# The first chunks of four batches at once, loaded by four-token rows, in a recurrence-and-expert kernel

## The chip, the cores and the metric

The kernel runs on one core of a Trainium2 chip. The metric is the device time of one execution in microseconds (us). The same kernel, run again, mostly agrees within a few tenths of a per cent. On some chips of this study it spread more, so every experiment was run beside the kernel before on its own chip, and the ratio to those runs counts. An execution over 1.5% longer than the fastest of its kernel is called slow, any other fast. The trace of one execution is read beside it. Its span, from the first to the last instruction, is mostly 1.7 to 2 us shorter than the device time (2.9 at most in these runs).

Engines: PE is TensorE (matmuls), DVE VectorE, ACT ScalarE, POOL GpSimd. SP issues transfers ("the sync queue"), and ACT and GpSimd have queues of their own.

## The reference, cut to what matters

```python
B, H, S, D = 4, 8, 768, 48            # float32 inputs; alpha in 0.8 .. 1.0
for t in range(S):
    state = alpha[:, :, t, :, None] * state + einsum('bhd,bhe->bhde', k[:, :, t], v[:, :, t])
    y[:, :, t] = einsum('bhd,bhde->bhe', q[:, :, t], state)
x = y.transpose(0, 2, 1, 3).reshape(3072, 384)
h = x @ w_in                           # 384 -> 2048
r = maximum(h, 0); out = (r * r) @ w_out   # 2048 -> 384
```

First comes a gated linear recurrence over time for each batch and head, then an expert layer with squared ReLU over all 3072 tokens.

## The kernel before

The recurrence is cut into chunks of 128 tokens, six for each batch, 24 in all. Within a chunk, cumulative products of alpha (a logarithm on ACT, a triangular matmul on PE, two exponentials on ACT) scale q and k. Masked scores times v give the part within the chunk, and a state carried from chunk to chunk gives the rest. The expert layer's matmuls keep PE busy from some 22 us on, and the later chunks are woven between them by a small scheduler that fixes the order of all instructions when the kernel is built.

The kernel before starts with the first four chunks of batch 0. Their alpha and q come in rows of four tokens (192 floats, 768 B) into tiles of 128 partitions, two transfers for each; k and v come chunk by chunk:

```python
slot_srcs = {n: a[0, :, 0:4 * P, :].rearrange("h (p j) d -> p h (j d)", j=4) for n, a in srcs}
LB = 5; LBV = 6                                   # buffers of the later tiles
...
def load_slots(nm, lo, hi):                       # half of the heads, all 128 partitions
    nc.sync.dma_start(out=slot[nm][:, lo:hi], in_=slot_srcs[nm][:, lo:hi])
...
def load_tile(nm):                                # v is cast to bf16 on its way in
    if nm == "vt": return loads.tile([P, H, D], BF16, name=nm, bufs=LBV)
    return loads.tile([P, H, D], FP32, name=nm)
... (nc.gpsimd if pool or nm == "vt" else nc.sync).dma_start(out=d[nm], in_=src[b, c])
...
def e_ps():                                       # state += kI^T v, chunk after chunk
    for p in range(NP): mm(st[:, p, :], lhsT=kI[:, 2*p:2*p+2, :], rhs=d["vt"][:, 2*p:2*p+2, :], ...)
def e_stm(): nc.vector.tensor_mul(st4, st4, bcast(ae, D))
def e_sb():  nc.scalar.copy(d["sbt"], d["st"])
...
def e_out(): nc.sync.dma_start(out=out_r[GT[g] + tt], in_=box["ob"])     # one transfer a tile
```

## Time and profile before

| | before |
|---|---|
| device time, median of the first three runs | 191.22 us (190.83 to 191.79) |
| span of the trace | 189.4 us |
| first expert matmul | 22.50 us |
| last expert matmul ends | 186.29 us |
| PE from the one to the other ("the stream") | 163.8 us |
| output after it ("the tail") | 3.1 us |

Three stretches add up to the span: the fill, the stream and the tail. The prediction below shows the lines for them. One more line belongs here, the granted clock of PE in 40 slices of 4.7 us (9 is full speed):

```profile
PEclk9998589999999999999999999999999999999999
```

The clock is low once, in the fourth to sixth slices, at the end of the fill.

### The profile page before, as it was taken

Reading aid. Unit: us, or ns where it says so; the run is one execution under the profiler, and the core shown is the slowest. Engines: PE = TensorE matmul, PEld = TensorE weight load, DVE = VectorE, ACT = ScalarE, POOL = GpSimd, SP = SyncE. Lnnn points to the kernel's source line nnn. Section 1 sums busy time; section 2 is a strip of 40 time slices with the busy share of each in tenths; the row PEclk is TensorE's granted clock in tenths of the full one; section 3 lists DMA queues with packets and bytes.
Section 4 is the critical chain, followed back from the end, with each engine's and each line's share of the span. In section 5 each row is a group of like instructions: output and inputs, shape, how many; then the busy total and the mean of one; then the engine's idle time right before and its main releaser. Section 6 shows DMA issues by size and latency. Waiting matters only on the chain.

```text
span 189.4 us, 5215 instructions
## 1 busy us (share of the span) xinstructions
PE 180.2 (95%) x1999; PEld 137.1 (72%) x1999; DVE 132.3 (70%) x335; ACT 126.7 (67%) x346; POOL 42.2 (22%) x78
## 2 busy tenths in 40 slices
PE   7864999999999999999999999999999999999993
PEld 2553778866878887777777787787787787777773
DVE  3167946754899795897886886886886886944411
ACT  3763459926778886678588588488588586565630
POOL 8967335023122233222021031041000000000000
PEclk9998589999999999999999999999999999999999
DMA  5999999899999999999959739739011011011112
GB/s 177 238 165 203 204 223 211 125 183 147 183 191 185 206 180 173 201 153 188 218 130 142 166 84 124 170 87 126 0 45 43 3 42 45 6 37 45 42 42 83
DMA packets 94280, 24.71 MB, mean 130 GB/s; under 512 B 85216, under 2 KB 93920, under 8 KB 94256
## 3 DMA queue, kind: packets, MB, share of 16 engines
q1 hardware_dynamic: 64992, 17.45, 44.8%
q0 software_dynamic: 29120, 6.88, 37.5%
q8 instruction: 15, 0.25, 0.6%
q14 instruction: 9, 0.07, 0.1%
q10 hardware_dynamic: 144, 0.05, 0.1%
HBM read 25.17 MB, written 4.72 MB: 158 GB/s over the span
## 4 chain that ended last, share of the span: by engine, by line
PE 87%; DMA 5%; SPq 3%; ACT 1%; DVE 1%; issue 1%; ACTq 0%; DVEq 0%
PE bank L226 78%; PE bank L229 7%; DMA kt<-in_k_dram 5%; PE st L226 2%; SPq L339 2%; SPq L319 1%; ACT r L668 1%; DVE st L578 1%; DVE sm L533 1%; ACT sb L583 0%; ACT xn L220 0%; DVE ob L736 0%; ACT ob L736 0%; ACT L_s L442 0%; DVE kI_s L474 0%
## 5 line engine op out<-in xcount | busy, mean ns | idle before, releaser
L668 ACT ACTIVATE r<-bank 128x256 bf16<-128x256 f32 (+1 forms) x160 | 64.7, 429 | 29.6 <-PE bank L226 28.2
L226 PE MATMUL bank<-xT_big,w_in_b 128*128 128x256 bf16 (+1 forms) x624 | 80.0, 266 | 0.1
L226 PE MATMUL bank<-w_out_b,gT 128*128 128x384 bf16 (+1 forms) x400 | 74.7, 320 | 0.0
L226 PEld LDWEIGHTS <-w_in_b 128*128 128x128 bf16 x624 | 53.8, 98 | 9.7 <-issue 0.5
L675 DVE TENSOR_TENSOR gT<-r 128x256 bf16<-128x256 bf16 (+1 forms) x160 | 47.6, 315 | 16.0 <-ACT r L668 14.4
L226 PEld LDWEIGHTS <-gT 128*128 128x128 bf16 x400 | 37.9, 98 | 15.8
L533 DVE TENSOR_TENSOR sm<-bank,utri_b 128x512 bf16<-128x512 f32 x40 | 25.3, 683 | 2.6 <-PE bank L226 2.5
L339 POOL DMA_DIRECT2D vt<-in_v_dram x24 | 21.3, 888 | 7.9 <-POOL vt L338 6.1
L338 POOL CAST vt<-kt 128x1 bf16<-128x1 f32 x18 | 4.7, 263 | 64.6 <-PE bank L226 41.8
L471 DVE TENSOR_TENSOR qA_s<-qt,A 128x384 bf16<-128x384 f32 x20 | 11.1, 556 | 9.5 <-ACT A L458 8.6
L218 DVE COPY qkT<-bank 128x1024 bf16<-128x1024 bf16 x20 | 13.8, 688 | 4.9 <-PE bank L229 4.9
L474 DVE TENSOR_TENSOR kI_s<-kt,Ainv 128x384 bf16<-128x384 f32 x24 | 13.3, 556 | 3.1 <-DMA kt<-in_k_dram 2.6
L709 ACT COPY ob<-bank 128x384 f32<-128x384 f32 x21 | 10.1, 480 | 8.1 <-PE bank L226 8.1
L226 PEld LDWEIGHTS <-qkT 64*128 64x128 bf16 (+1 forms) x260 | 10.4, 97 | 5.9 <-issue 2.5
L220 ACT CAST xn<-bank 128x384 bf16<-128x384 f32 x23 | 10.9, 480 | 4.2 <-PE bank L226 3.8
L583 ACT CAST sb<-st 128x384 bf16<-128x384 f32 x20 | 9.6, 478 | 5.7 <-DVE st L578 5.7
L458 ACT ACTIVATE A<-bank 128x384 bf16<-128x384 f32 x20 | 9.9, 496 | 2.4 <-PE bank L226 2.4
L229 PE MATMUL bank<-ident_bf,kI_s 128*128 128x128 bf16 x96 | 9.5, 223 | 2.1 <-DVE kI_s L474 2.1
L578 DVE TENSOR_TENSOR st<-st,ae_s 128x384 f32<-128x384 f32 x20 | 11.1, 556 | 0.0
L442 ACT ACTIVATE L_s<-at 128x384 bf16<-128x384 f32 x20 | 10.4, 521 | 0.0
L462 ACT ACTIVATE Ainv<-bank 128x384 bf16<-128x384 f32 x20 | 10.2, 510 | 0.0
L229 PE MATMUL bank<-ident_bf,qA_s 128*128 128x128 bf16 x96 | 9.3, 219 | 0.8 <-DVE qA_s L407 0.7
(78 smaller groups left out, 162.1 us busy)
## 6 DMA issues: line engine op xcount, KB each, us to landing
out_dram<-ob SPq DMA_DIRECT2D x23, 192.0 KB, 2.7
kt<-in_k_dram SPq DMA_DIRECT2D x21, 192.0 KB, 5.3
at<-in_alpha_dram SPq DMA_DIRECT2D x18, 192.0 KB, 4.8
qt<-in_q_dram SPq DMA_DIRECT2D x18, 192.0 KB, 4.7
vt<-in_v_dram POOLq DMA_DIRECT2D x24, 96.0 KB, 5.6
w_in_b<-in_moe_w_in_dram POOLq DMA_DIRECT2D x4, 384.0 KB, 11.0
w_out_b<-in_moe_w_out_dram POOLq DMA_DIRECT2D x4, 384.0 KB, 12.3
slot_at<-in_alpha_dram SPq DMA_DIRECT2D x2, 384.0 KB, 3.6
```

Source lines behind the costliest of these rows:

```text
L218: pin(nc.vector.tensor_copy(out, in_))
L220: pin(nc.scalar.copy(out, in_))
L226: pin(nc.tensor.matmul(*a, **kw))
L229: pin(nc.tensor.transpose(*a))
L339: pin((nc.gpsimd if pool or nm == "vt" else nc.sync).dma_start(out=d[nm], in_=src[b, c]))
L442: pin(nc.scalar.activation(L[:, :, 0:D], d["at"], AF.Ln))
L471: pin(nc.vector.tensor_mul(qA[:, :, 0:D], d["qt"], d["A"]))
L474: pin((nc.vector if mk.eng == "DVE" else nc.gpsimd).tensor_mul(kI[:, :, 0:D], d["kt"], d["Ai"]))
L533: pin(nc.vector.tensor_mul(d["sm"][:, hh], d["sc"][hh], (utri_p if first else utri_b).to_broadcast([P, NP, P])))
L578: pin(nc.vector.tensor_mul(st4, st4, bcast(ae, D)))
L668: pin(nc.scalar.activation(box["r"], box["ph"], AF.Relu))
L675: pin(nc.vector.tensor_mul(gT[g][:, f0:f0 + nf, 0:n], box["r"], box["r"]))
```

## The change

The four first chunks are now those of all four batches, which do not depend on each other, so the chain of states drops out of the fill. Alpha, q and k come with one transfer a batch, by four-token rows, and each batch fills 32 partitions. Scores are made for two batches by halves of the heads. After that the kernel goes batch by batch. The new token order of the first tiles is kept through to the output, which is put right by four output transfers a tile. The core of the diff (names, masks, scheduling ranks and most of the arithmetic cut):

```diff
-    slot_srcs = {n: a[0, :, 0:4 * P, :].rearrange("h (p j) d -> p h (j d)", j=4) for n, a in srcs}
+    NJ, PQ = 4, 32
+    rows = {n: a[:, :, 0:P, :].rearrange("b h (g j) d -> b g h (j d)", j=NJ) for n, a in srcs}
+    v_rows = v[:, :, 0:P, :].rearrange("b h (g j) d -> j g (b h) d", j=NJ)
+    SEQ = [(b, 0) for b in range(B)] + [(b, c) for b in range(B) for c in range(1, NCH)]
-    LB = 5
-    LBV = 6
+    LB = 4
...
+    def load_batch(nm, b, q, at):
+            pin(q.dma_start(out=slot[nm][b * PQ:(b + 1) * PQ], in_=rows[nm][b]))
+    def load_v(j, at):
+            pin(nc.sync.dma_start(out=v_0[j * PQ:(j + 1) * PQ]..., in_=v_rows[j]))
...
+    def load(s, pool):                     # later chunks: v in float32 too, on the same queue
+        for nm in ("at", "qt", "kt", "vt"):
+                pin((nc.gpsimd if pool else nc.sync).dma_start(out=C[s][nm], in_=srcs[nm][c, :, ...]))
...
+        def e_vb():                        # and cast by GpSimd
+            pin(nc.gpsimd.tensor_copy(d["vb"], d["vt"]))
...
-            pin(nc.sync.dma_start(out=out_r[GT[g] + tt], in_=box["ob"]))
+            if SEQ[GT[g] + tt][1] == 0:
+                for j in range(NJ):
+                    pin(nc.sync.dma_start(out=out_tile(GT[g] + tt)[j], in_=ob[j * PQ:(j + 1) * PQ]))
...
+    ld_at = [load_batch("at", b, nc.sync if b % 2 == 0 else nc.scalar, 0.9) for b in range(B)]
+    ld_qt = [load_batch("qt", b, nc.sync, 1.7) for b in range(B)]
+    ld_kt = [load_batch("kt", b, nc.sync, 1.7) for b in range(B)]
+    def hold():                            # the weights wait for the last k
+        pin(nc.gpsimd.tensor_copy(w_in_b[3 * PQ:P, 0, 0:1], slot["kt"][3 * PQ:P, 0, 0:1]))
```

## The prediction

> **What bounds the kernel now.** I read four views of the kernel before, in this order. First the page's shares of the chain of waits that ended last:
>
> ```profile
> PE 87%; DMA 5%; SPq 3%; ACT 1%; DVE 1%; issue 1%; ACTq 0%; DVEq 0%
> ```
>
> PE carries 87% of the chain, so most of the kernel cannot be shortened by taking a wait away. The chain in order of time tells where the other 13% lie (columns: start us, us, what):
>
> ```profile
> 3.47 2.81 SPq L339
> ...
> 6.33 9.01 DMA kt<-in_k_dram
> ...
> 15.84 0.56 DVE st L578
> 16.40 0.96 DVE sm L533 x2
> ...
> 18.09 0.49 ACT sb L583
> ...
> 22.50 15.27 PE bank L226 x139
> ```
>
> Up to 15.3 us the path is the third key tile's transfer; then comes the serial chain over the four chunks of batch 0 (state update on DVE, its copy on ACT, the next state matmul on PE), until 22.50 us. From there on the chain is PE with hardly a break to 186.31 us; 3.1 us of output follow. Third, the windows (stretch, length, busy us of PE, PEld, DVE, ACT, POOL, granted clock, DMA share, GB/s):
>
> ```profile
> 12.00:14.00 2.00, 1.23 (x20) 0.97 (x20) 1.23 (x3) 1.26 (x4) 0.77 (x1) 1.00 1.63 162
> 14.00:16.00 2.00, 0.57 (x14) 0.26 (x10) 0.64 (x2) 0.09 (x1) 1.46 (x2) 1.00 1.38 192
> 18.00:20.00 2.00, 1.84 (x20) 1.29 (x17) 2.00 (x5) 1.00 (x3) 0.75 (x1) 0.50 1.24 203
> 22.00:24.00 2.00, 1.99 (x25) 1.54 (x23) 1.91 (x4) 0.86 (x3) 0.76 (x1) 0.50 1.30 202
> 30.00:35.00 5.00, 5.00 (x51) 4.42 (x50) 3.06 (x8) 4.65 (x9) 1.28 (x2) 1.00 1.28 219
> ```
>
> PE starves at 14 to 16 us, its clock is then halved (second by second from about 17.9 to 24.7 us), and after that PE is full. Fourth, the timeline, where the first expert matmul and the speed of the stream are seen:
>
> ```profile
> 22.50 0.80 PE L226 MATMUL bank<-xT_big,w_in_b 128*128 128x256 bf16 x3
> ...
> 27.51 7.38 PE L226 MATMUL bank<-xT_big,w_in_b 128*128 128x256 bf16 x66
> ```
>
> So the time is: start of the expert stream (22.50) + work of PE from there (163.8) + tail (3.1) = 189.4 us of span; the device time of 191.22 lies 1.8 above it. The change can win only by an earlier start, less PE work in the stream, or fewer cold cycles.
>
> **What the Trainium skill says.** "TensorE: Matmul & The Clock Gate", Part 1, gives two states of the clock, half and full, switched by a free-running activity window of 3.4 us, and a warm matmul spacing of N/2.4 + 2.5 ns. The trace agrees: clock exactly 0.50 for 6.7 us (two windows), and 66 matmuls of 256 columns in 7.38 us less one drain, about 109 ns each. "DMA: Bandwidth & Descriptors", Specifications, asks for 512 B or more per piece; the trace shows 366 GB/s at 3 to 4 us with 768 B rows and 158 to 174 at 9 to 13 us with 192 B rows and casts. The same page's "Queues, rings and completion order" says that each DMA engine takes turns between the queues with work; the third key tile, issued at 6.33, landed only at 15.34 while GpSimd's queue was busy, which fits. "SBUF — State Buffer", "Door 1: The DMA port swizzle", says 32 (or 64) neighbouring partitions reach 8 of 16 ports. The new transfers are of 32 partitions each; no transfer of before is, so the trace cannot test it. It may cost them their speed where two of the same half run together.
>
> **The change part by part.**
>
> *Loads.* Alpha, q and k of all four first chunks come in 768 B rows, 4 x 196 KB each, 2.36 MB; v in 192 B rows, 0.79 MB, uncast. The weights are held until the last k landed. Two of the four alpha transfers are issued by ACT behind its table load (0.80 to 2.08 us). Before, an alpha transfer landed 3.3 to 4.0 us after issue, so all four are there at about 5.4 (before: 5.3). The queue on SP reuses eight semaphores, so each k transfer waits for an alpha and each v for a q to land. At 250 to 300 GB/s (estimate from the trace's 257 to 366 at 3 to 7 us, lowered for the ports) k is complete at 2.2 + 2.36/0.27 = 11 us, before 15.3. Then v at about 200 GB/s needs 4 us alone; from about 13 us the first weights share with it: v lands at about 16.5 to 17, the first quarter of w_in (393 KB) at about 17.
>
> *ACT.* From 5.4: 4 logarithms of 0.52 and 8 exponentials of 0.50 make 6.1 us, last one at 11.5. Before it was two of 0.84 and the same eight, ended 10.25.
>
> *DVE.* Its multiplies (0.556 each, 8) start when A of pair 0 is ready, 5.4 + 2.1 + 0.5 = 8.0, and are limited by ACT to about 13.3. Two copies of 0.375 make 14.0. Then the masks: eight halves of 256 columns. A 512-column one takes 0.683 and a 384-column multiply 0.556, about 1 ns a column, so 0.43 for 256, some 0.38 apart: batches 0 and 1 are done at 17.1, batches 2 and 3 (4 x 0.64) at 19.7. No state chain stands in this path any more: about 5 us of before's chain (15.3 to 20.5) go.
>
> *ACT and PE to the first expert matmul.* ACT casts v of batches 0 and 1 (2 x 0.48) when v has landed: 17.8. Second batch's value product 0.4, cast 0.5, three transposes 0.35, copy 0.5, and 0.1 to 0.2 of latency each: 20.0. That is the predicted start, 2.5 us before the old one. From the order of instructions, its first matmul needs x of both batches 0 and 1, so v and the masks for batch 1 are what ends last.
>
> *Work in the stream.* Counting the columns of all matmuls from the first expert matmul on, in the order of instructions: before 1826 with 373,968 columns, after 1854 with 377,552. At 2.4 columns/ns and 2.5 ns each that is 160.4 and 162.0: 1.6 us more. It comes from moved state matmuls of four first chunks, 16 transposes that bring the keys back by tokens, and state products for all later chunks. The measured 163.8 had 1.1 of cold clock (22.5 to 24.65 at half) and 2.3 of other gaps.
>
> *Clock.* The new fill gives PE little to do between 9.5 and 20 us (transposes, scores), so I expect one cold spell again, ending up to a window after the dense stream begins: 1.5 us lost instead of 1.1, 0.4 more.
>
> *Elsewhere.* v is now cast by GpSimd, 20 later tiles (nobody waits for GpSimd's time today: 22% busy). DVE takes some key copies, with 70% busy. Outputs of four tiles become four transfers each on SP. All beside PE.
>
> *Sum.* -2.5 + 1.6 + 0.4 = -0.5, so 190.7; I put it at 190.5, as GLA's four chunks no longer depend on each other and small waits on state go with them.
>
> **The rivals.**
>
> 1. *v and weights land late.* If the two queues share evenly from 12 us, v lands at 19 and the start moves to 22.3; with the extra work that gives about 193. For it: the 9 us of the third key tile. Against: v is ahead of the weights by the hold.
> 2. *The next chunk's alpha becomes the wait.* The order has the logarithm of the fifth chunk after only four ReLUs (before: after twelve), some 4 to 5 us behind the start. ACT is in order: if that tile is not there at about 25 us (4.9 MB have to come first: 11 + 2.56 MB at 205 GB/s = 23.5), ReLUs stop and PE with them. Each us late is a us lost; up to 194.
> 3. *All goes as planned.* k at 9, v at 14.5, no cold spell: then DVE's masks bind, start about 18.8, no cold loss: 191.2 - 3.7 + 1.6 - 1.1 = 188.0. For it: transfers at over 300 GB/s for 768 B rows in the trace. It still does not reach -2%.
> 4. *GpSimd's casts block DVE.* They read SBUF at the same time as squares on DVE; before has only one-element casts (0.26 us). DVE has 30% slack, so below 0.5 us in the end.
>
> **Range and chances.** The centre is 190.5. Early landing gives 188, late v or late fifth chunk 193 to 194; 8 in 10 in 188.0 to 193.0. Faster by over 2% needs under 187.4, which takes a start near 17 us, earlier than DVE's row of masks allows: 0.07. Slower by over 2% (over 195.0) needs two of the rivals at once: 0.06. Within: 0.87.
>
> **What would show it.** Right: the first expert matmul at 19 to 21.5 us; the chain before it through v or DVE's masks, no state step; PE without break after it; clock 0.50 somewhere between 13 and 24 us; last expert matmul about 165 to 166 us after the first. k landed by 12 us. Wrong: a chain that goes through ACT's logarithm of the fifth chunk at 24 to 30 us; a first expert matmul after 22.5 or before 18; PE's stream longer than 167 us (a new wait in it) or shorter than 163.5 (gaps of before gone, which I did not count).

## The result, and the profile after

| | before | after |
|---|---|---|
| device time, median of 4 runs | 191.38 us (190.83 to 191.79) | 197.94 us (197.15 to 200.03) |
| ratio | | 1.036 (1.028 to 1.045) |
| span of the profiled run | 189.4 | 198.3 |
| first expert matmul | 22.50 | 23.51 |
| stream | 163.8 | 171.7 |
| tail | 3.1 | 3.1 |

The change made the kernel 3.6% slower. A ratio in this document is the mean time of one kernel's fast runs over that of the kernel before in the same rounds, so it is not quite the ratio of the medians quoted; the brackets are 95% intervals. The profiled run of after is the slowest of its four, by 2.1 us, and its mean clock is the lowest (0.947; the others 0.956, 0.974 and 0.957), so its cold spells are longer than those of the other runs, and its waits may be.

The granted clock now, in slices of 5 us, and the shares of the chain that ended last:

```profile
PEclk9985579999999995799999999999999999999999
...
PE 83%; DMA 9%; ACT 3%; DVE 2%; SPq 1%; issue 1%; DVEq 0%
```

There is a second cold spell in the middle, where before had none, and transfers hold 9% of the chain instead of 5%. The chain in order of time shows both places. First the fill:

```profile
1.28 5.80 DMA slot_at<-in_alpha_dram
...
7.10 7.55 DMA slot_kt<-in_k_dram
...
15.40 2.02 PE bank L208 x16
...
18.98 1.43 DVE sm L587 x4
...
22.60 0.87 ACT xT_big L199 x2
...
23.51 0.80 PE bank L205 x3
```

The states are gone from it, as intended. But alpha ends at 7.08 and k at 14.65, so everything behind them, up to the first expert matmul, is late. The rates of the first transfers tell why (the SP view of the windows: stretch, length, clock, DMA share, GB/s), first before:

```profile
3.00:4.00 1.00, 1.00 1.08 366
5.00:6.00 1.00, 1.00 0.93 257
6.00:7.00 1.00, 1.00 1.00 303
```

then after:

```profile
3.00:4.00 1.00, 1.00 1.15 257
5.00:6.00 1.00, 1.00 1.12 196
6.00:7.00 1.00, 1.00 1.15 218
```

The engines are at least as busy as before (shares of 1.12 to 1.15 against 0.93 to 1.08) and move 24% to 30% less, with rows just as long. v, behind k in the same queue, is late too: ACT's cast of it, which waits for it, starts at 18.78.

```profile
18.78 0.92 ACT L199 CAST vb<-v 128x384 bf16<-128x384 f32 x2 [0.74 <-DMA v<-in_v_dram]
```

It ends at 19.70, and the masks of batches 0 and 1 on DVE at 20.41, so the masks are what the path waits for last, by 0.7 us. Then the middle of the stream, again the chain:

```profile
64.72 0.56 DVE kI_s L530
...
66.44 0.72 SPq L775
...
69.09 4.39 DMA at<-in_alpha_dram
...
73.51 0.52 ACT L_s L503
...
75.70 0.50 PE bank L208 x3
```

and the sync queue at that time:

```profile
66.44 2.12 SPq L775 DMA_DIRECT2D out_dram<-ob  x4
68.65 0.40 SPq L434 DMA_DIRECT2D vt<-in_v_dram  x1
69.09 0.59 SPq L434 DMA_DIRECT2D at<-in_alpha_dram  x1
```

Line 775 is the output by four transfers. It keeps the queue for 2.12 us, then comes a v tile, and only then the alpha tile, which lands at 73.48. ACT's logarithm waits for it, the ReLUs wait behind the logarithm because ACT works in order, and PE waits for them (windows: stretch, length, busy us of PE, PEld, DVE, ACT and POOL, clock, DMA share, GB/s):

```profile
70.00:75.00 5.00, 1.90 (x22) 1.05 (x19) 0.96 (x4) 1.49 (x4) 0.51 (x1) 0.99 0.83 165
75.00:80.00 5.00, 4.30 (x26) 3.13 (x27) 3.31 (x8) 2.15 (x7) 0.55 (x1) 0.50 0.91 192
```

PE stands from 71.9 to 75.7 (PE's waits after 24 us: us in total, times, longest):

```profile
PE bank L208 <- ACT xn L199: 3.8, 1, 3.8
```

The clock is 0.50 from 74.9 to 81.7.

The account of the stream, 171.7 - 163.8 = 7.9 us more: the wait 3.8; half clock from the end of the wait at 75.7 to 81.7, 3.0; half clock at the start, 23.5 to 27.1, 1.75 where before lost 1.1, so 0.65; more PE work, 1.6 as counted in the prediction. That is 9.05, so some 1.2 us of small gaps that before has must have gone; I did not trace them. With the start, 1.0 us later, the span grows by 8.9.

So there are two questions: why does PE stand in mid-stream, and why is the fill slower instead of faster?

### The profile page after: what moved, and what is told of

The parts are those of the page before. It is cut to its first block, busy times and chain, and to the rows that moved or that the text cites. A ratio compares the mean times of both kernels' runs of the same rounds, so it can differ in the third digit from the quotient of the medians.

```text
span 198.3 us, 5294 instructions
## 1 busy us (share of the span) xinstructions
PE 184.3 (93%) x2011; PEld 140.9 (71%) x2011; DVE 132.4 (67%) x338; ACT 130.5 (66%) x355; POOL 31.4 (16%) x61
## 4 chain that ended last, share of the span: by engine, by line
PE 83%; DMA 9%; ACT 3%; DVE 2%; SPq 1%; issue 1%; DVEq 0%
PE bank L205 72%; PE bank L208 9%; DMA slot_kt<-in_k_dram 4%; DMA slot_at<-in_alpha_dram 3%; DMA at<-in_alpha_dram 2%; PE st L205 2%; SPq L775 1%; DVE sm L587 1%; ACT r L721 1%; ACT xT_big L199 0%; ACT xn L199 0%; SPq L434 0%; ACT Ainv L518 0%; DVE gT L728 0%; DVE qk_f L364 0%
## 5 line engine op out<-in xcount | busy, mean ns | idle before, releaser
L205 PE MATMUL bank<-xT_big,w_in_b 128*128 128x256 bf16 (+1 forms) x624 | 81.7, 269 | 0.2 <-ACT xT_big L199 0.2
L205 PE MATMUL bank<-w_out_b,gT 128*128 128x384 bf16 (+1 forms) x400 | 76.2, 323 | 0.0
L728 DVE TENSOR_TENSOR gT<-r 128x256 bf16<-128x256 bf16 (+1 forms) x160 | 48.7, 326 | 17.4 <-ACT r L721 15.8
L496 POOL CAST vb<-vt 128x384 bf16<-128x384 f32 x20 | 12.1, 604 | 100.4 <-PE bank L205 61.5
L767 ACT COPY ob<-bank 128x384 f32<-128x384 f32 x23 | 11.0, 478 | 10.5 <-PE bank L205 10.4
L208 PE MATMUL bank<-ident_bf,xn 128*128 128x128 bf16 x72 | 8.6, 238 | 4.1 <-ACT xn L199 4.1
L530 DVE TENSOR_TENSOR kI_s<-kt,Ainv 128x384 bf16<-128x384 f32 x20 | 11.1, 554 | 0.7 <-ACT Ainv L518 0.5
L208 PEld LDWEIGHTS <-xn 128*128 128x128 bf16 x72 | 5.7, 106 | 6.1 <-ACT xn L199 4.6
L197 DVE COPY xT_big<-bank 128x384 bf16<-128x384 bf16 x21 | 7.3, 350 | 3.9 <-PE bank L208 3.8
L205 PE MATMUL bank<-vb,sm 128*128 128x48 bf16 x192 | 9.1, 189 | 0.0
```

Of the source, the lines that this page charges most:

```text
L197: pin(nc.vector.tensor_copy(out, in_))
L205: pin(nc.tensor.matmul(*a, **kw))
L208: pin(nc.tensor.transpose(*a))
L496: pin(nc.gpsimd.tensor_copy(d["vb"], d["vt"]))
L530: pin(nc.vector.tensor_mul(kI[:, :, 0:D], d["kt"], d["Ai"]))
L728: pin(nc.vector.tensor_mul(gT[g][:, f0:f0 + nf, 0:n], box["r"], box["r"]))
```

## The experiments

Sixteen kernels ran. Each was correct unless said otherwise. Ratios use fast runs alone; the medians and ranges quoted are of all runs, slow ones included (one of the first two-queue form, seven of the kernel before with split outputs, two of the kernel before with idle matmuls, and some of the kernel before itself). A single run has no state and is used for its trace alone. The stream, the start and the waits are from the profiled run of each, and they vary: two of the experiments below (five buffers; later v by GpSimd) leave the fill as it is in the changed kernel, and their k lands at 14.35 and 14.31 instead of 14.65 and their first expert matmul comes at 23.21 and 22.74 instead of 23.51. Differences of less than 0.8 us between the starts of two traces show nothing.

### Why PE stands in mid-stream

**Token order restored, so that each tile leaves in one transfer.** The copy of x into the expert's input puts the first tiles back in token order.

```diff
-            copy(d["x"], xT_big[:, :, s * P:(s + 1) * P], d["px"])
+            xo, xi = xT_big[...], d["px"]
+            if first:
+                xo, xi = xo.rearrange("p k (g j) -> p k j g", j=NJ), xi.rearrange("p k (j g) -> p k j g", j=NJ)
+            copy(d["x"], xo, xi)
-        return rows.rearrange("(g j) n -> j g n", j=NJ) if c == 0 else rows
+        return rows
```

> One part undone: the four first-chunk tiles leave in one output transfer each, not four (the copy of x writes the columns in token order, so the result stays right). Theory A (the stall at 72 to 76 us comes from the sync queue, which issues in order and spends 1.7 to 2.8 us on each group of four outputs ahead of the next alpha load): PE's idle 3.8 us at 72 to 76 us and the cold spell after it (6.4 us at half clock, 3.2 us lost) go, and the time falls from about 198 to 191 to 193 us. Rival B (four load buffers instead of five set when the loads are issued): the stall stays and the time is within 1 us of the changed kernel.

Measured: 194.61 us (193.86 to 194.97), ratio 1.017 (1.010 to 1.025). The wait and the second cold spell are gone:

```profile
70.00:75.00 5.00, 4.99 (x58) 3.69 (x57) 4.61 (x12) 3.60 (x10) 0.51 (x1) 1.00 0.95 209
```

The stream is 165.7 us, 1.9 above before: just the predicted extra work and cold clock (1.6 and 0.4). The time stays above the 191 to 193 expected: the fill is as late as before the edit. The strided copy costs 0.94 us instead of 0.43, and the first expert matmul is at 24.07.

**Five buffers for the later loads** (and three instead of four for the transposed q and k, to make room). The rival was that alpha is late because its buffer is.

```diff
-    loads = ctx.enter_context(tc.tile_pool(name="loads", bufs=LB))
+    loads = ctx.enter_context(tc.tile_pool(name="loads", bufs=LB + 1))
```

> The other part undone: five buffers for every later alpha, q, k and v tile, as before for alpha, q and k (one buffer of the transposed tile is given up for room; the order of instructions stays). Rival B: the stall at 72 to 76 us goes and the time falls to 191 to 193 us. Theory A: the outputs still stand in front of the loads, so less than half of it goes, 195 us or more.

Measured: 197.97 us (196.2 to 198.34), ratio 1.032 (1.017 to 1.047); PE still waits 2.8 us. The time is that of the changed kernel, so the number of buffers alone is not the cause.

**The kernel before with the first four tiles' outputs split in four.**

```diff
-            pin(nc.sync.dma_start(out=out_r[GT[g] + tt], in_=box["ob"]))
+            for j in range(NJ if g < 2 else 1):
+                pin(nc.sync.dma_start(out=out_r[GT[g] + tt][j * w:(j + 1) * w], in_=box["ob"][j * w:(j + 1) * w]))
```

> One suspected cost put into the kernel before: its first four output tiles leave in four transfers of 32 rows each. Theory A in its strong form (the split outputs alone make a stall): 2 to 6 us slower than before. If the split hurts only together with fewer load buffers and with v on the same queue: within 1 us of before.

Measured: 191.74 us (median of 20 runs), ratio 0.9985 (0.995 to 1.002). The profiled run is of the slow state (197.82 us, first expert matmul at 28.28), so only its queue is read:

```profile
54.16 1.91 SPq L716 DMA_DIRECT2D out_dram<-ob  x4
```

The four transfers take the queue nearly as long as in after (1.76 to 2.17 us against 1.74 to 2.84). PE waits nowhere in its stream, but with so late a start the loads had more time; that the split alone does no harm here rests on the ratio of the fast runs. So my theory lacked a half. One thing that differs on that queue is a fourth load a chunk: the change moved v there.

**After, with the later v tiles issued by GpSimd** (same bytes, same order of instructions; split outputs kept).

```diff
-                pin((nc.gpsimd if pool else nc.sync).dma_start(out=C[s][nm], ...))
+                pin((nc.gpsimd if pool or nm == "vt" else nc.sync).dma_start(out=C[s][nm], ...))
```

> The changed kernel with one thing altered: the v tiles of the later chunks are issued by GpSimd's queue instead of the sync queue (same bytes, same rows, same order of instructions); the four output transfers per first-chunk tile stay on the sync queue. In the kernel before, the same split outputs cost nothing, and its sync queue carried three loads a chunk, not four. Theory A2 (the stall needs both: four loads a chunk and the split outputs on one in-order queue): the PE wait near 72 us shrinks below 1 us and the time falls to 194.5 to 195.5. Rival (the split outputs alone make the stall here): PE still waits 2.5 us or more, time 197 to 198.5.

Measured: 193.78 us (193.53 to 194.04), ratio 1.015 (1.011 to 1.019), the fastest correct form of the changed kernel. Its queue and PE:

```profile
67.34 2.20 SPq L775 DMA_DIRECT2D out_dram<-ob  x4
```

```profile
70.00:75.00 5.00, 4.99 (x55) 3.68 (x54) 4.58 (x12) 3.56 (x11) 3.07 (x2) 1.00 0.96 200
```

The outputs still block the queue for 2.2 us, but PE never waits after 24 us, and the stream is 165.8. Some 0.8 us of the gain in this trace is its earlier start (22.74), which the edit does not touch. In the changed kernel the stall needs both, four loads a chunk and four outputs a tile on one queue in order: taking either away ends it.

**Token order by a matmul** with a permuted identity, as the kernel before has it, instead of the strided copy.

```diff
+                if first:
+                    mm(d["px"][:, j, :], lhsT=d["xn"][:, j * P:(j + 1) * P], rhs=ident_by_token, start=True, stop=True)
+                    continue
```

> As the one-output-transfer run, but x is put in token order by a matmul with the permuted identity (as in the kernel before) and not by a strided copy, which took 0.9 us a tile. Theory A: no stall at 72 to 76 us and a first expert matmul at about 23.5 us, so 193.5 to 194 us, up to 1 us below the strided copy's 194.4. If the copy was not on the path: 194.4 again.

Measured: 195.17 us (194.54 to 196.11), above the 193.5 to 194 expected, ratio 1.019 (1.009 to 1.030), first expert matmul at 24.02, stream 165.5. Within the intervals it is the same as the strided copy: ACT saves half a microsecond a tile, and in this trace PE's six matmuls for two tiles take 1.48 us at half clock.

### Why the fill is slow

**Halves of the partitions in two queues**: batches 0 and 1 on the sync queue, 2 and 3 on ACT's (alpha, q) and GpSimd's (k).

```diff
-    ld_qt = [load_batch("qt", b, nc.sync, 1.7) for b in range(B)]
-    ld_kt = [load_batch("kt", b, nc.sync, 1.7) for b in range(B)]
+    ld_qt = [load_batch("qt", b, nc.sync if b < 2 else nc.scalar, 1.7) for b in range(B)]
+    ld_kt = [load_batch("kt", b, nc.sync if b < 2 else nc.gpsimd, 1.7) for b in range(B)]
```

> The first q and k loads on two queues, batches 0 and 1 (partitions 0 to 63) on the sync queue and batches 2 and 3 (partitions 64 to 127) on the ScalarE queue for alpha and q, on GpSimd's for k. Theory C (transfers to 32 partitions that follow one another in one queue reach only half of the ports, about 210 GB/s): 280 to 350 GB/s between 3 and 9 us, alpha landed at about 6 instead of 7.1 us, k at 11 to 12 instead of 14.7 us, first expert matmul at 20.5 to 21.5 instead of 23.5 us, time 2 to 3 us less than the changed kernel. Rival D (the rate is that of 32-partition transfers however they are mixed, or of HBM): still about 210 GB/s, and the time within 1 us.

Measured: 197.86 us (195.33 to 199.53), ratio 1.030 (1.011 to 1.050). Rates at 3 to 8 us are 333, 247, 247, 240 and 254 GB/s. Alpha landed at 6.5 and q was used at 9.7 (in the changed kernel 7.1 and 11.0), but k still at 14.6, and the first expert matmul at 23.01 is within the spread of unchanged fills. Whether k is held by sharing the engines with v through GpSimd's queue is what the next run tests.

**The same with k's second half on ACT's queue.**

```diff
+    ld_kt = [load_batch("kt", b, nc.sync if b < 2 else nc.scalar, 1.7) for b in range(B)]
```

> The run on two halves again, with k of batches 2 and 3 on the ScalarE queue too, so that no GpSimd queue shares the engines with v before k is in. Theory C (a queue of 32-partition transfers in a row reaches half of the ports): 250 to 330 GB/s from 3 to 10 us, k landed at 11 to 12.5 us (changed kernel 14.7), first expert matmul at 20.5 to 22 us, time 1.5 to 3 us below the changed kernel. Rival D (32-partition transfers are slow however mixed): k at 14 us or later, time within 1 us of the changed kernel.

Measured: 198.16 us (197.68 to 198.82), ratio 1.036 (1.027 to 1.044), alpha at 6.33, k at 14.24, first expert matmul at 23.10. Rates at 4 to 8 us are 236 to 263, in the changed kernel 196 to 220. Mixing the halves raises the rate by some 20%; on k, which ACT issues behind its logarithms (6.5 and 7.9 us), it gains nothing beyond the spread (14.31 and 14.35 with the old fill). The expectation of 11 to 12.5 failed, so GpSimd's queue was not what held k, and what did in this form is open.

**The kernel before with its first tiles brought by 32-partition transfers.** Same bytes, same rows, same queue; each tensor comes in four transfers of 32 partitions and 192 KB instead of two of 128 and 384 KB. (The logarithms then wait for all four alpha transfers, so the time is not comparable.)

```diff
-                pin(nc.sync.dma_start(out=slot[nm][:, lo:hi]..., in_=slot_srcs[nm][:, lo:hi]))
+        for r in (0, 1, 2, 3)[:2] if lo == 0 else (0, 1, 2, 3)[2:]:
+                w = slice(r * PQ, (r + 1) * PQ)
+                pin(nc.sync.dma_start(out=slot[nm][w]..., in_=slot_srcs[nm][w]))
```

> The kernel before with its first alpha and q tiles (the same bytes, rows of 768 B, one queue) brought by four transfers of 32 partitions each, in the order 0, 1, 2, 3, instead of two over 128 partitions. Theory C (transfers that lie in one half of the partitions are slow): 200 to 230 GB/s at 3 to 6 us where before has 366, 301 and 257; alpha complete 1 us or more later than before's 5.26. Rival (the transfers of the changed kernel are slow for another reason, such as two queues or strided batches): 280 GB/s or more at 3 to 6 us, alpha at 5.2 to 5.6. The end of the kernel may be somewhat later in both, as the logarithms wait for all four.

```profile
3.00:4.00 1.00, 1.00 1.07 187
5.00:6.00 1.00, 1.00 1.09 210
6.00:7.00 1.00, 1.00 1.11 217
```

Measured: 195.24 us in one run. The rate falls from 366, 257 and 303 to 187, 210 and 217 (the changed kernel: 257, 196 and 218). Nothing but the shape was altered, which here includes the number and size of the transfers; the next run keeps those.

**The same in the order 0, 2, 1, 3**, so that neighbours in the queue lie in different halves.

> As the run before it, with only the order of the four transfers changed to 0, 2, 1, 3, so that neighbours in the queue lie in different halves of the partitions. Theory C: the rate at 3 to 6 us rises again to 250 GB/s or more. If the queue works one transfer off at a time, the order does not matter and it stays at 200 to 230. Rival (not the partitions): 280 or more in both orders.

```profile
3.00:4.00 1.00, 1.00 1.11 191
5.00:6.00 1.00, 1.00 0.99 263
6.00:7.00 1.00, 1.00 1.12 237
```

Measured: 193.81 us in one run. From 5 to 8 us the rate is higher by 20 to 53 GB/s, with as many transfers of the same size, so which partitions are under way together matters there. At 3 to 5 us (191 and 204) it is not higher, against the expectation: the order accounts for part of the loss, and the rest is not divided between fewer partitions and smaller transfers.

**One transfer per head over all 128 partitions**, on the form with token order by matmul and idle matmuls (next part), with v held until k has landed.

```diff
+    def load_head(nm, h, q, at):
+            pin(q.dma_start(out=slot[nm][:, h], in_=rows[nm][:, :, h]))
+    ld_at = [load_head("at", h, nc.scalar if h % 2 else nc.sync, 0.9) for h in range(H)]
+    ld_qt = [load_head("qt", h, nc.gpsimd if h % 2 else nc.sync, 1.7) for h in range(H)]
+    ld_kt = [load_head("kt", h, nc.sync, 1.7) for h in range(H)]
```

> The run with token order by matmul and idle matmuls, but alpha, q and k of the first chunks come as one transfer per head over all 128 partitions (98 KB each) instead of one per batch over 32, and v waits for the last k. Theory C (the fill is late because transfers of 32 partitions run slowly): 270 GB/s or more at 3 to 8 us, alpha complete at 5.5 to 6.2, k at 10.5 to 12.0, first expert matmul 20.0 to 21.5, time 191.5 to 193.0 (194.5 with transfers by batch and half). Rival F (v and the first weights set the start, not k): k earlier, first expert matmul still at 22.5 or later, time 194 to 195. Rival G (the supply of the later chunks bounds the stream): start earlier, but PE idle after the start grows by as much, time 193.5 to 194.5.

Measured: 220.63 us, ratio 1.158. All three theories missed:

```profile
12.00:14.00 2.00, 0.50 0.28 80
```

The DMA share is 0.28, that is 4.5 of 16 engines, and 80 GB/s. The Trainium skill, "DMA: Bandwidth & Descriptors", section "Why a DMA increments its semaphore by 16 and not by 1", has the reason under "How many engines": the number of engines is the largest up to 16 that divides the slowest dimension of both sides. The source of these transfers has the four batches as its slowest dimension, so four engines; the trace's 0.28 agrees. I had not looked it up, and the run says nothing on the 32-partition shape. A form that reaches all partitions and all engines was not run.

**v held until k has landed**, in the form with two queues.

```diff
+        pin(nc.gpsimd.tensor_copy(v_0[:, 0, 0, 0:1], slot["kt"][:, H - 1, 0:1]))   # v's transfers wait for this
```

> As the run with halves on the scalar queue, token order by matmul and idle matmuls, with one thing more: the four v transfers wait until the last k has landed. Theory C with sharing: at the 236 to 263 GB/s measured for mixed halves k is complete at 12.5 to 13.2 instead of 14.25, v at 17 to 18, first expert matmul 21.5 to 22.3, time 193.0 to 194.0. Rival F: v lands later than before (19 or more) and the first expert matmul stays at 23.0 or later, time 194.3 or more.

Measured: 207.65 us, ratio 1.089. k landed at 13.20, as expected. But v:

```profile
15.76 16.79 DMA v<-in_v_dram
```

The weights and the next tiles were issued by GpSimd from 14.7 us on. v, issued from 13.95 to 17.7, landed at 32.55. The first expert matmul came at 37.7. The rival named the direction, by no means the size. In the changed kernel v, issued ahead of the weights, is safe; behind them it is not.

**Half of k and v left out** (the other partitions filled with a constant; wrong on purpose), in the form with two queues, token order by matmul and idle matmuls.

> The run with halves on the scalar queue, token order by matmul and idle matmuls, but only two of the four k transfers and two of the four v transfers of the first chunks; the other partitions are filled with a constant, so the result is wrong on purpose. Theory (the start follows the transfers of k and v one to one): k complete at 12.2 to 13.0 (14.25 without), v at 15.5 to 17, first expert matmul at 21.0 to 21.9 (23.09 without), time 192.0 to 193.3 (194.5 without). Rival (ScalarE and VectorE set the start): first expert matmul at 22.5 or later, time 194.0 or more. If the start comes earlier and the time does not, the supply of the later chunks takes the gain: PE idle or late after the start by that much.

Measured: 195.72 us, ratio 1.024, first expert matmul at 26.7. The scheduler counts transfers, and with fewer of them it put a q product behind k's: DVE did that one at 17.03, and the masks began at 19.71 instead of 17.22. The test was spoilt by its own edit.

**The same, with the order of all instructions kept** (the scheduler still counts the transfers, which are not issued).

```diff
+            if nm != "kt" or b % 2 == 0:
                 pin(q.dma_start(out=slot[nm][b * PQ:(b + 1) * PQ], in_=rows[nm][b]))
```

> As the run with half of k and v, but the order of all instructions is that of the run with halves on the scalar queue, token order by matmul and idle matmuls (in the first attempt the scheduler, told of fewer transfers, put the last q product behind the k products and so confounded it). The result is wrong on purpose again. Theory (the start follows the transfers of k and v one to one): k complete at about 13.2, the first four masks done at 18.2 to 18.6 (19.47 without), v in time, first expert matmul at 21.8 to 22.3 (23.09 without), time 193.2 to 193.8 (194.5 without). Rival (another wait, such as the first weights or the next chunk, takes the gain): first expert matmul at 22.8 or later, or the same time of 194.3 to 194.8 with more PE idle after the start.

Measured: 192.25 us (20 runs, 191.02 to 193.72), ratio 1.004 (1.002 to 1.007). DVE's products with k, and then PE:

```profile
12.97 1.97 DVE L367 TENSOR_TENSOR qk_f<-slot_kt,Ainv 128x384 bf16<-128x384 f32 x4 [0.78 <-DMA slot_kt<-in_k_dram]
```

```profile
21.70 0.49 PE L206 MATMUL bank<-xT_big,w_in_b 128*128 128x256 bf16 x3 [0.36 <-ACT xT_big L200]
```

With all bytes those were at 14.37 and 23.09. The products come 1.40 earlier and the first expert matmul 1.39 earlier: the start follows the transfers of k and v one to one. (Both are halved, so the run does not say which of them; in the changed kernel it was k, by 0.7 us.) The time falls by 2.25 us, more than the start, because a PE wait of 1.0 us at 70 to 80 us goes as well.

### Does the cold clock cost anything?

**Idle matmuls in the waits of the fill** (27 of them), on the form with token order by matmul.

```diff
+    fill = {"t0": 8, "t1": 9, "p22": 6, "p30": 4}
+            for _ in range(fill.pop(at)):
+                mm(wp, lhsT=warm[:, 0:P], rhs=warm[:, 0:NP * 2 * D], start=True, stop=True)
```

> The run before with 27 idle matmuls of 384 columns put into PE's waits of the fill (before the first q and the first k transposes, before the second pair of scores and before the first value product), on the state's bank, which is unused until then. Theory E (the cold clock from 13.5 to 27 us costs PE-bound time and slows the fill): clock 1.00 from 14 to 27 us, stream start 0.5 to 1 us earlier and 1.5 to 2 us of half-speed stream gone: 191 to 192 us. Rival: the clock drops anyway, or the fill is not PE-bound: within 0.7 us of the run without them.

Measured: 195.2 us (194.37 to 196.75), ratio 1.021 (1.011 to 1.030). The clock is 1.00 throughout and the first expert matmul 0.4 earlier, and the time is the same as without. So the rival is right. The chain now leads through a transfer of the fifth chunk:

```profile
21.78 9.65 DMA kt<-in_k_dram
```

and PE waits 1.5 us for an alpha tile near 72 us. Without them the clock was 0.62 on average from 20 to 30 us, 3.8 us lost, of which 2.0 lie before the first expert matmul and 1.8 behind it. Those 1.8 are given back: 1.7 shows as PE waits, and the stream is 166.5 us instead of 165.5, of which 1.1 I could not assign.

**The same with the two queues.**

> All three together: one output transfer a tile, loads of the two halves on two queues, idle matmuls in the fill. If the three costs add up: 197.9 - 3.9 (outputs) - 2 (loads) - 2 (clock) = 190 us, at or just below the kernel before. If the loads only move the wait to v or to the masks on DVE: 191.5 us or more.

Measured: 194.5 us (194.13 to 195.2), ratio 1.017 (1.009 to 1.025), first expert matmul at 23.09, one PE wait of 1.0 us near 73 us. The three costs do not add up to the 190 us of the expectation.

**Idle matmuls in the fill of the kernel before** (11 of them). This was the candidate to beat both.

```diff
+            n = {"p12": 6, "ps1": 3, "p23": 2}.get(getattr(op, "key", None), 0)
+            if n and op.dur:
+                dummies(n, op.start - 0.5, op.start)
```

> The kernel before with eleven idle matmuls in the three PE waits of its fill (14 to 19 us), which do nothing but keep PE busy. Theory E (half clock costs the kernel before something): clock 1.00 throughout, the 1.1 us lost after 22.50 come back, 190.0 to 190.5. Rival: the half-clock matmuls stand beside other work or the idle matmuls delay others: 191.0 to 192.0, ratio 1.000 within 0.002.

Measured: 190.68 us (14 runs) against 191.22 us (19 runs), ratio 0.999 (0.996 to 1.002). The trace is 0.9 us shorter, at full clock:

```profile
18.00:20.00 2.00, 1.58 (x23) 1.05 (x23) 2.00 (x5) 0.90 (x3) 0.88 (x1) 1.00 1.24 204
```

but the interval includes no gain at all. No version here beats the kernel before.

## Why the prediction was wrong

It said 190.5 us and within 2%. It was 197.94 and slower by 3.6%. Taken step by step:

**"At 250 to 300 GB/s ... k is complete at ... 11 us" failed.** It was 14.65, and alpha landed at 7.1 instead of 5.4. The rate from 4 to 13 us was 196 to 220 GB/s. The estimate rested on before's transfers of 128 partitions. The prediction cited the Trainium skill, "SBUF — State Buffer", section "Door 1: The DMA port swizzle", that 32 neighbouring partitions reach only half of the ports, and put it aside with a small allowance "for the ports". The same section's table has a rate for it: 189 GB/s for one transfer of 1 MiB to partitions 0 to 31, against 328 to all 128. The run on the kernel before with this shape shows 187 to 217 against 257 to 366, about a third less, not a tenth; with 200 GB/s in the prediction's sum k would have been expected at 2.2 + 2.36/0.2 = 14.0. v, behind k, was late with it: its cast started at 18.78, where the prediction has v landed at 16.5 to 17. That this made the start 3.5 us later than predicted is supported by the run with half of k and v, in which the start moves with them one to one.

**The length from k to the first expert matmul came out, in part by luck.** Predicted 9.0 us (11 to 20.0), measured 8.86 (14.65 to 23.51). But the prediction had DVE held by ACT until 13.3, not by k, and v's cast end last, at 17.8, with 2.2 us from there; measured, DVE waited for k, the masks ended last, at 20.41, and 3.1 us followed. The states did drop out of the fill. The one intended gain was real and smaller than the loss in front of it.

**"Outputs of four tiles become four transfers each on SP ... All beside PE" failed.** This, together with "PE without break after it", is the larger error against the kernel before: a wait of 3.8 us and 3.0 us of half clock behind it in the profiled run, and by the medians 3.3 us when the split is undone (197.94 to 194.61) and 4.2 when v's loads leave the queue (193.78). The split alone costs nothing on the kernel before (ratio 0.9985). The prediction gave these transfers no time at all, and did not ask in which order one queue must issue them just before a tile that ACT needs.

**Rival 2 had the right mechanism at the wrong place.** It was ACT in order behind a logarithm that waits for alpha, but at 72 us and because of the queue, not at 25 us because of the bytes. Rival 1 came nearly true: v landed just before 18.78, where it says 19, but mostly because k, ahead of it in the queue, was 3.65 us late; what sharing with the weights added was not separated. It did not bind only because the masks of batches 0 and 1, at 20.4, ended 0.7 us after v's cast, at 19.7. Had k alone been on time and v landed as it did, v would have bound: 19.7 + 3.1 = 22.8, an estimate from this trace.

**"1.6 us more" of PE work agrees, as a part of a sum.** Without the stall the stream is 165.5 to 165.8 us in three runs, 1.7 to 2.0 above before, against a predicted 1.6 for work and 0.4 for the clock.

**The clock of the fill** came as predicted, half speed from about 13.4 to 27.1 us, 1.75 us lost against 1.5. What was not predicted is that buying it back gains nothing: in the changed kernel without its stall the chain then leads through the transfers of the next chunks, and in the kernel before the ratio is 0.999.

**The sum as it should have been:** with the start at 23.5, +1.0; PE work, +1.6; clock of the fill, +0.65; the wait in mid-stream and the cold spell behind it, +3.8 and +3.0: 10.05 against a span that grew by 8.9; the 1.2 us left over are not found in the trace. "Slower by over 2% needs two of the rivals at once" was right as a sentence; the second was one that I had set down as harmless.

## What to carry to other kernels

When a transfer keeps its bytes and rows but is cut to fewer partitions, take its rate from a transfer of that shape, not from the wide one. When a change adds transfers to a queue that issues in order, follow that queue by itself through the moment when a tile that an engine in order needs is next. And when an experiment takes work away from a kernel whose order is made by a scheduler, keep the scheduler's picture as it was, or the order changes with the work.

## What the Trainium skill lacked or had wrong

- "SBUF — State Buffer", "Can I just issue two DMAs to hit both halves?", says that two transfers to the two halves at once gained only 6% over one. Here the gain was larger: 236 to 263 GB/s at 4 to 8 us with the halves in two queues, against 196 to 220 with the batches in order, and 231 to 263 at 5 to 8 us with alternating halves in one queue, against 195 to 217. It is still short of the 257 to 303 that 128 partitions had at 4 to 7 us.
- "DMA: Bandwidth & Descriptors", "Queues, rings and completion order", says that an engine takes turns between queues, but not how much a queue of short rows can lose beside others: v in 192 B rows, 0.79 MB, was issued at 13.95 to 17.7 us and landed only at 32.55, with GpSimd's weights and tiles under way from 14.7. That taking turns is the cause was not tested.
- I found on no page a measured time, on this chip, for which several small transfers in a row hold the queue that issues them: 1.74 to 2.84 us for four of 48 KB here, in which the queue issues nothing else.
